# Favor attention and two expert layers on one core: the later units' projections by heads, with the high and the low part stacked in the partitions

## Chip, core and metric

The kernel runs on one core of a Trainium2 chip. The metric is the device time in microseconds (us) of one execution; lower is better. The engines are named as in the profile: PE is TensorE's matmul side and PEld its weight loads, DVE is VectorE, ACT ScalarE, POOL GpSimd, SP the queue from which most transfers are issued.

## The reference

Three stages follow each other; the second and third take the first one's result. Only the first is touched. Inputs q, k, v have 4 batches, 8 heads, 576 tokens and 64 numbers per token and head; omega is 128 x 64.

```python
def phi(x):                                   # x: q or k, times 64 ** -0.25
    proj = np.einsum('bhsd,md->bhsm', x, omega)
    sq = np.sum(x * x, axis=-1, keepdims=True) / 2.0
    h = proj - sq
    h = h - np.max(h, axis=-1, keepdims=True)
    return np.exp(h) / np.sqrt(m)
q_p, k_p = (phi(q_s), phi(k_s))
kv = np.einsum('bhsm,bhsd->bhmd', k_p, v)
z = np.sum(k_p, axis=2)
num = np.einsum('bhsm,bhmd->bhsd', q_p, kv)
den = np.einsum('bhsm,bhm->bhs', q_p, z)[..., None] + 1e-06
return (num / den).astype(np.float32)
```

After it come a gated layer over all 2304 tokens (512 to 1536 to 512) and a layer of 8 experts (512 to 1024 to 512) in which each token goes to one expert.

## The kernel before

Attention is cut into 72 units: one unit is 128 tokens of q or of k, four heads each. The first 16 units ("start") and the next 14 are put in order by a planner (`Plan`); the 42 after them, the later units, are not planned: `start_unit` puts their steps into a list of tasks with due times (`T.at`, `SOFFS`), and the loop of the gated layer (`moe1_group`, `T.step`) lets each task out between its own products. So a later unit's products stand in TensorE's queue among the long products of the gated layer: `gv`, 384 columns, and `acc`, 512 columns. The order is fixed when the program is built.

The steps of a unit are made by `unit_stages`. `s1` transposes the 128 tokens by two matmuls (a transpose takes two heads of 64 numbers, so the result has two heads above each other in the 128 partitions) into the PSUM tile `xt`, [128, 2, 128]. To keep float32 precision with the faster rounded type (F32R), `s1b` copies `xt`, rounded, to `xh` on ScalarE, and `s1x` subtracts it from `xt` on VectorE, which leaves the low part `xl`. `s1c` makes the sums of squares. `s2` is the projection: for each pair of heads, `mm3` (lines 186 to 189) issues three products, high by high, high by low, low by high:

```python
o = pr[:, 2 * a:2 * a + 2, :].rearrange("p h m -> p (h m)")
mm3(o, xh[:, a, :], xl[:, a, :], om_h, om_l, True, True)
```

Since a pair has two heads in the partitions, `om_h` and `om_l` (128 x 256, the high and low part of omega) hold omega twice: in partitions 0 to 63 for the columns 0 to 127, in partitions 64 to 127 for the columns 128 to 255, and zeros elsewhere. A pair's products have 256 columns, and half of what they multiply is zeros. `s2b` (maximum, VectorE) and `s2c` (exponential, ScalarE) read the result `pr`; the rest of a unit (`s3...`, `s4...`, `s5...`) is the attention itself. `xt`, `pr`, `qt`, `num` and `xot` of later units share two PSUM buffers (`misc`); `xh` and `xl` have one buffer each.

Units are numbered from 0 to 71 here; unit 30 is the first later one. Each later unit's `s2` issues 6 products of 256 columns.

Of the kernel before, what the change touches and what calls it, by code (L numbers as in the profile page):

```python
# [8 lines left out]
F32 = mybir.dt.float32  # L9
F32R = mybir.dt.float32r  # L10
I32 = mybir.dt.int32
ACTF = mybir.ActivationFunctionType
ALU = mybir.AluOpType
# [46 lines left out]
P = 128  # L60
# [79 lines left out]
def kernel(  # L140
# [16 lines left out]
    nc = tc.nc  # L157
# [25 lines left out]
    def misc(shape, name):  # L183
        return psum.tile(shape, F32, tag="misc", name=name, bufs=2)

    def mm3(o, lh, ll, rh, rl, start, stop):
        nc.tensor.matmul(o, lh, rh, start=start, stop=False, skip_group_check=True)  # L187
        nc.tensor.matmul(o, lh, rl, start=False, stop=False, skip_group_check=True)  # L188
        nc.tensor.matmul(o, ll, rh, start=False, stop=stop, skip_group_check=True)  # L189
# [11 lines left out]
    with tc.manual_schedule():  # L201
        upool = ctx.enter_context(tc.tile_pool(name="upool", bufs=2))
        tpool = ctx.enter_context(tc.tile_pool(name="tpool", bufs=1))
        attn = attn_stack.enter_context(tc.tile_pool(name="attn", bufs=1))
# [62 lines left out]
        def load_x(n, x):  # L267
            kind, t, j = units[n]
            src = q if kind == "q" else k
            for r, m, b, s in segs(t):  # L270
                nc.sync.dma_start(out=x[r:r + m],
                                  in_=src[b, 4 * j:4 * j + 4, s:s + m, :].rearrange("h s d -> s h d"))
# [30 lines left out]
        def pump():  # L303
            while nload[0] < len(units) and room["xin"]:
                n = nload[0]
                room["xin"] -= 1
                loads[n] = attn.tile([P, 4, D], F32, tag="xin", name="xin", bufs=3)
                load_x(n, loads[n])
                nload[0] += 1
                if not planning:  # L310
                    pump_v()
            if not planning:
                pump_v()

        def pump_v():
            while nload[1] < nload[0]:
                n = nload[1]
                kind, t, j = units[n]
                if kind == "k":
                    nv = 1 + edge(t)  # L320
                    if room["vin"] < nv:
                        return
                    room["vin"] -= nv
                    vt = [attn.tile([P, 4, D + 2], F32, tag="vin", name="vin", bufs=2) for _ in range(nv)]
                    vals[n] = [x.rearrange("p (h b) d -> p h b d", b=2) for x in vt] if nv > 1 else vt[0]
                    load_v(n, vals[n])
                nload[1] += 1
# [16 lines left out]
        def first_tile(n):  # L344
            if n not in first:
                first[n] = wpool.tile([P, 1024], F32, tag="w", name="first")
            return first[n]
# [17 lines left out]
        def first_part(src, j, u):  # L365

            hp, rp = divmod(u, 2)
            return quad[src, j][:, 2 * hp:2 * hp + 2, 2 * rp:2 * rp + 2, :]
# [49 lines left out]
        om_h = const.tile([P, 2 * P], F32R, name="om_h")  # L418
        om_l = const.tile([P, 2 * P], F32R, name="om_l")
# [23 lines left out]
        def wsteps(key):  # L443

            st = {}


            def a():
                st["r"] = wraw.pop(key)
                st["t"] = rows.tile([P, DM], I32, tag="row", name="wt")  # L450
                nc.vector.tensor_scalar(out=st["t"], in0=st["r"][:, :, 1], scalar1=3, scalar2=0x3FFFFFFF,
                                        op0=ALU.logical_shift_left, op1=ALU.bitwise_and)

            def b():
                nc.vector.scalar_tensor_tensor(out=st["t"], in0=st["r"][:, :, 1], scalar=-0x40000000, in1=st["t"],
                                               op0=ALU.bitwise_and, op1=ALU.bitwise_or)

            def c():
                nc.vector.scalar_tensor_tensor(out=st["t"], in0=st["r"][:, :, 0], scalar=29, in1=st["t"],
                                               op0=ALU.logical_shift_right, op1=ALU.bitwise_or)  # L460

            def d():
                wch[key] = wpool.tile([P, 2, DM], F32R, tag="w", name="w")
                nc.scalar.copy(wch[key][:, 0, :], st["t"].bitcast(F32))

            def e():
                nc.vector.tensor_tensor(out=wch[key][:, 1, :], in0=st["t"].bitcast(F32),
                                        in1=wch[key][:, 0, :].bitcast(F32), op=ALU.subtract)

            return a, b, c, d, e  # L470
# [8 lines left out]
        def unit_stages(i):  # L479
            kind, t, j = units[i]  # L480
            x_none = kind == "k" and t < 4
            st = {}
            start = i < n_start
            planned = i < n_start + n_grp[0]
            accum = not start and planned

            def bank(shape, name):
                if i < n_start and name in ("xt", "xot"):
                    return psum.tile(shape, F32, tag="gv", name=name, bufs=2)
                if i < n_start and name == "pr":  # L490
                    return psum.tile(shape, F32, tag="acc", name=name, bufs=GT)
                return misc(shape, name)

            def s1():
                if start:
                    u = first_tile(i)
                    x = loads.pop(i, None)
                    xh = u[:, 4 * D:8 * D].rearrange("p (a t) -> p a t", t=P)
                    h = u[:, 8 * D:8 * D + 4 * M].rearrange("p (h m) -> p h m", m=M)
                else:  # L500
                    x = loads.pop(i)
                    h = attn.tile([P, 4, M], F32, tag="h", name="h", bufs=2)
                    xh = attn.tile([P, 2, P], F32R, tag="xh", name="xh", bufs=1)
                xl = None
                xt = bank([P, 2, P], "xt")
                if x is None:
                    part = first_part("k", j, t)
                    pair = [part[:, a].rearrange("p r d -> p (r d)") for a in range(2)]
                    hsq, xsq = h[:, :, 0:D].rearrange("p (a r) d -> p a r d", a=2), part
                else:  # L510
                    pair = [x[:, 2 * a:2 * a + 2, :].rearrange("p h d -> p (h d)") for a in range(2)]
                    hsq, xsq = h[:, :, 0:D], x
                for a in range(2):
                    nc.tensor.transpose(xt[:, a, :], pair[a], ident)
                ss = attn.tile([P, 4], F32, tag="ss", name="ss", bufs=4)
                st.update(x=x, xh=xh, h=h, ss=ss, xt=xt, pair=pair, sq=(hsq, xsq))

            def s1b():
                nc.scalar.copy(st["xh"], st["xt"])

            def s1x():
                xl = st["xl"] = attn.tile([P, 2, P], F32R, tag="xl", name="xl", bufs=1)
                nc.vector.tensor_tensor(out=xl, in0=st["xt"], in1=st["xh"].bitcast(F32), op=ALU.subtract)

            def s1c():
# [14 lines left out]
            def s2():  # L540
                xh, xl = st["xh"], st.get("xl")
                pr = st["pr"] = bank([P, 4, M], "pr")
                for a in range(2):
                    o = pr[:, 2 * a:2 * a + 2, :].rearrange("p h m -> p (h m)")
                    if start:
                        nc.tensor.matmul(o, xh[:, a, :], om_f, start=True, stop=True)
                    else:
                        mm3(o, xh[:, a, :], xl[:, a, :], om_h, om_l, True, True)
# [111 lines left out]
            def s5c():  # L660
                nc.vector.tensor_tensor(out=st["o"][1], in0=st["xo"], in1=st["o"][0].bitcast(F32), op=ALU.subtract)  # L661
                if not start:
                    freed("xin")

            parts = dict(T=s1, xh=s1b, xl=s1x, sq=s1c, pj=s2, rd=s2b, ex=s2c)
            if start:
                parts = dict(T=s1, xh=s1b, sq=s1c, ss=s1d, sc=s1e, pj=s2, rd=s2b, md=s2m, ex=s2c)
            elif accum:
                parts = dict(T=s1, xh=s1b, xl=s1x, sq=s1c, pj=s2, rd=s2b, md=s2m, ex=s2c)
# [87 lines left out]
        for g, n2, n3 in ((0, 4, 2), (1, 1, 1), (2, (NT - E) // (2 * P) + E, 0)):  # L757
            r = Round()
# [588 lines left out]
        for n, key in enumerate(worder):  # L1347
            load_chunk(n)
            st = wsteps(key)
# [113 lines left out]
        fin[3].extend(x for x in plan.todo if x[0] != "end")  # L1463
        plan.run(fin)
        planning.clear()
        pump()
        TG = NF * (4 * 0.98 + 3 * 0.65)
        p0 = T.now - TG
# [15 lines left out]
        st = slot_prefetch(A, A.slots[0], tf + PF, PD, tf + FR[0][0] * 12 + FR[0][1] + 1.4 + PG)  # L1484
        moe1_group(NG - 1)
        cur = pending[0]
        for i, (r, s) in enumerate(slots):
# [4 lines left out]
            st = nst  # L1492
# [53 lines left out]
```

## Time and profile before

| | us |
|---|---|
| median of 2 runs (872.6 to 872.7) | 872.65 |
| the profiled execution, its own time | 873.23 |
| its span, from the first to the last instruction | 871.30 |
| PE busy | 851.5 (98%) |
| PEld busy | 788.1 (90%) |
| DVE busy | 599.1 (69%) |
| ACT busy | 369.3 (42%) |

The profile's rows come from one profiled execution. Busy time of PE is the union of its products' durations; they overlap, because a product's row runs until its last result is written while the next one has long begun. What a product costs in a row of products is the distance between two starts. A weight load (LDWEIGHTS) brings a product's stationary operand into the array, and each product has one.

### The profile page before, as it was taken

To read this page: it belongs to the slowest core of one execution; us is meant where nothing else is said; L and a number is where in the kernel's file an instruction comes from. 1 tells how busy PE (TensorE), PEld (TensorE's weight loads), DVE (VectorE), ACT (ScalarE), POOL (GpSimd) and SP (SyncE) were. 2 spreads that over 40 slices of the span, in tenths; PEclk is the share of its full clock that TensorE was granted. 3 is DMA by queue.
4 is the path that set the end of the run, shared out by engine and by line. 5 is a ranking of instruction groups with operands and counts; after the bars stand their busy time and mean duration, and the time that the engine had idled before them with its cause. 6 is when DMAs were issued, how large, how long until landed. Compare 5 with 4: busy or idle time off the path is not lost. (4 is left out here: it accounts for less than half of the span.)

```text
span 871.3 us, 14616 instructions
## 1 busy us (share of the span) xinstructions
PE 851.5 (98%) x5115; PEld 788.1 (90%) x5115; DVE 599.1 (69%) x1581; ACT 369.3 (42%) x1024; POOL 101.0 (12%) x236
## 2 busy tenths in 40 slices
PE   7899999999999999999999999999999999999994
PEld 6789889999999999999999999999999999999994
DVE  6999899466665666566666665488887777976520
ACT  4857665334333434243443331211374445555420
POOL 6812200000000000000000000000112014321010
PEclk9999999999999999999999999999999999999998
DMA  8926641222213112141112211131767654776000
GB/s 254 277 76 183 215 140 43 76 50 59 63 46 111 38 42 55 43 133 43 37 43 77 51 32 37 57 113 46 260 220 278 200 182 140 253 246 233 25 27 25
DMA packets 89389, 98.68 MB, mean 113 GB/s; under 512 B 53504, under 2 KB 55570, under 8 KB 89307
## 3 DMA queue, kind: packets, MB, share of 16 engines
q1 hardware_dynamic: 85995, 87.90, 33.0%
q0 software_dynamic: 3040, 9.70, 3.2%
q8 instruction: 42, 0.69, 0.3%
q14 instruction: 40, 0.33, 0.1%
q10 hardware_dynamic: 272, 0.07, 0.0%
HBM read 84.26 MB, written 13.65 MB: 112 GB/s over the span
## 5 line engine op out<-in xcount | busy, mean ns | idle before, releaser
L187 PE MATMUL gv<-xT,w 128*128 128x384 f32 x576 | 201.4, 350 | 0.4 <-DVE xT L661 0.4
L189 PE MATMUL gv<-xT,w 128*128 128x384 f32 x576 | 193.9, 337 | 0.0
L188 PE MATMUL gv<-xT,w 128*128 128x384 f32 x576 | 193.5, 336 | 0.0
L187 PE MATMUL acc<-w,uh 128*128 128x512 f32 x352 | 143.6, 408 | 0.0
L189 PE MATMUL acc<-w,ul 128*128 128x512 f32 x352 | 138.8, 394 | 0.0
L188 PE MATMUL acc<-w,uh 128*128 128x512 f32 x352 | 138.7, 394 | 0.0
L578 ACT ACTIVATE h<-pr,mx 128x128 f32<-128x128 f32 x224 | 64.1, 369 | 145.1 <-DVE mx L573 133.4
L187 PEld LDWEIGHTS gv<-xT,w 128*128 128x128 f32 x576 | 108.4, 188 | 3.2 <-DVE xT L661 0.6
L188 PEld LDWEIGHTS gv<-xT,w 128*128 128x128 f32 x576 | 108.5, 188 | 2.4
L189 PEld LDWEIGHTS gv<-xT,w 128*128 128x128 f32 x576 | 108.1, 188 | 0.0
L788 DVE SCALAR_TENSOR_TENSOR wge<-xrow,wge 128x512 f32<-128x512 f32 x144 | 98.7, 685 | 11.4 <-DMA wge<-wg2t 10.7
L193 DVE TENSOR_TENSOR w<-raw,w 128x512 fp32r<-128x512 f32 x128 | 85.4, 687 | 3.2 <-ACT w L192 1.9
L189 PEld LDWEIGHTS acc<-w,ul 128*128 128x128 f32 x352 | 66.0, 188 | 14.6
L187 PE MATMUL h<-sx,w 128*128 128x256 f32 (+1 forms) x256 | 78.4, 306 | 0.0
L189 PE MATMUL h<-sx,w 128*128 128x256 f32 (+1 forms) x256 | 77.6, 303 | 0.0
L188 PE MATMUL h<-sx,w 128*128 128x256 f32 (+1 forms) x256 | 77.4, 302 | 0.0
L192 ACT CAST w<-raw 128x512 fp32r<-128x512 f32 x128 | 74.0, 618 | 2.0 <-DMA raw<-in_moe_w_dram 2.0
L188 PEld LDWEIGHTS acc<-w,uh 128*128 128x128 f32 x352 | 66.5, 189 | 7.5
L187 PEld LDWEIGHTS acc<-w,uh 128*128 128x128 f32 x352 | 66.4, 189 | 7.4
L560 DVE TENSOR_REDUCE mx<-pr 128x4 f32<-128x512 f32 x72 | 49.5, 687 | 22.9 <-PE pr L189 19.4
L1083 ACT CAST uh<-th 128x384 fp32r<-128x384 f32 x72 | 37.6, 522 | 63.6 <-DVE th L1078 62.3
L1074 DVE SCALAR_TENSOR_TENSOR th<-th,gv 128x384 f32<-128x384 f32 x72 | 39.7, 551 | 35.8 <-ACT th L1071 35.8
(232 smaller groups left out, 1409.3 us busy)
## 6 DMA issues: line engine op xcount, KB each, us to landing
raw<-in_moe_w_dram SPq DMA_DIRECT2D x64, 512.0 KB
wge<-wg2t SPq DMA_DIRECT2D x48, 256.0 KB
scr<-xrow SPq DMA_DIRECT2D x33, 256.0 KB
wraw<-in_moe_w_gate_dram SPq DMA_DIRECT2D x12, 512.0 KB
wraw<-in_moe_w_val_dram SPq DMA_DIRECT2D x12, 512.0 KB
wraw<-in_moe_w_out_dram SPq DMA_DIRECT2D x12, 512.0 KB
xin<-in_q_dram SPq DMA_DIRECT2D x26, 128.0 KB
xin<-in_k_dram SPq DMA_DIRECT2D x24, 128.0 KB
```

The lines of the kernel that those rows point to most:

```text
L187: nc.tensor.matmul(o, lh, rh, start=start, stop=False, skip_group_check=True)
L188: nc.tensor.matmul(o, lh, rl, start=False, stop=False, skip_group_check=True)
L189: nc.tensor.matmul(o, ll, rh, start=False, stop=stop, skip_group_check=True)
L192: nc.scalar.copy(hi, src)
L193: nc.vector.tensor_tensor(out=lo, in0=src, in1=hi.bitcast(F32), op=ALU.subtract)
L560: nc.vector.tensor_reduce(out=mx, in_=pr, axis=AX.X, op=ALU.max)
L578: nc.scalar.activation(out=h[:, a, :], in_=pr[:, a, :], func=ACTF.Exp, bias=mx[:, a:a + 1])
L788: nc.vector.scalar_tensor_tensor(out=st[e][:, 1, :], in0=xrows[i], scalar=1.0, in1=st[e][:, 0, :], op0=ALU.mult, op1=ALU.mult, accum_out=L ...
L1074: nc.vector.scalar_tensor_tensor(out=th[f], in0=th[f], scalar=1.0, in1=ps.pop((f, "g")), op0=ALU.add, op1=ALU.mult)
L1083: nc.scalar.copy(u[f][0], th[f])
```

## The change

The later units (not `planned`) get one tile `xs`, [128, 2, 2, 128], F32R. Its second axis is the place r of a head within the pair. For r = 0 the high part of the head in partitions 0 to 63 stays in partitions 0 to 63, and its low part is written to partitions 64 to 127; for r = 1 it is the other way round. So `xs[:, r, a, :]` holds one head, high and low above each other, and one product with omega's high part in both halves of the partitions gives (high + low) by omega's high part. `s1b` becomes two copies of 64 partitions, `s1x` two subtractions of 64 partitions whose result lies in the other half of the partitions, and `s2` eight products of 128 columns: for each of four heads one with `om_h` and one with `om_l`. For that, ScalarE copies omega's second block over the zeros beside it in `om_h` and `om_l` once, behind the planned part. The 30 units before keep their products; the 14 planned later ones only have `xh` and `xl` in the two halves of the new tile.

```diff
-                    xh = attn.tile([P, 2, P], F32R, tag="xh", name="xh", bufs=1)
+
+                    xh = st["xs"] = attn.tile([P, 2, 2, P], F32R, tag="xs", name="xs", bufs=1)
+                    if planned:
+                        xh = xh[:, 0]
...
             def s1b():
-                nc.scalar.copy(st["xh"], st["xt"])
+                if planned:
+                    nc.scalar.copy(st["xh"], st["xt"])
+                    return
+                for r in range(2):
+                    here = slice(64 * r, 64 * r + 64)
+                    nc.scalar.copy(st["xh"][here, r], st["xt"][here])
 
             def s1x():
-                xl = st["xl"] = attn.tile([P, 2, P], F32R, tag="xl", name="xl", bufs=1)
+                if not planned:
+                    for r in range(2):
+                        here, there = slice(64 * r, 64 * r + 64), slice(64 - 64 * r, 128 - 64 * r)
+                        nc.vector.tensor_tensor(out=st["xh"][there, r], in0=st["xt"][here],
+                                                in1=st["xh"][here, r].bitcast(F32), op=ALU.subtract)
+                    return
+                xl = st["xl"] = st["xs"][:, 1]
                 nc.vector.tensor_tensor(out=xl, in0=st["xt"], in1=st["xh"].bitcast(F32), op=ALU.subtract)
...
                 pr = st["pr"] = bank([P, 4, M], "pr")
+                if not planned:
+                    for a in range(2):
+                        for r in range(2):
+                            for n in range(2):
+                                nc.tensor.matmul(pr[:, 2 * a + r, :], xh[:, r, a, :], (om_h, om_l)[n][:, 0:P],
+                                                 start=n == 0, stop=n == 1)
+                    return
...
         planning.clear()
+
+        for om in (om_h, om_l):
+            nc.scalar.copy(om[64:128, 0:P], om[64:128, P:2 * P].bitcast(F32))
         pump()
```

The order of everything else on the five engines' queues is the same as before. Three places show what is new, all at unit 30. The first is TensorE's queue at its projection, between products of the gated layer (gv); before:

```order
L189 MATMUL gv<-xT_1604,w 128x384
L187 MATMUL pr<-om_h,xh 128x256 [waits DVE_49,Activation_49]
L188 MATMUL pr<-om_l,xh 128x256
L189 MATMUL pr<-om_h,xl 128x256 [waits DVE_49]
L187 MATMUL pr<-om_h,xh 128x256
L188 MATMUL pr<-om_l,xh 128x256
L189 MATMUL pr<-om_h,xl 128x256
L187 MATMUL gv<-xT_1604,w 128x384
```

And the same place of TensorE's queue with the change:

```order
L189 MATMUL gv<-xT_1594,w 128x384
L561 MATMUL pr<-om_h,xs 128x128 [waits DVE_49]
L561 MATMUL pr<-om_l,xs 128x128
L561 MATMUL pr<-om_h,xs 128x128 [waits DVE_49,Activation_49]
L561 MATMUL pr<-om_l,xs 128x128
L561 MATMUL pr<-om_h,xs 128x128
L561 MATMUL pr<-om_l,xs 128x128
L561 MATMUL pr<-om_h,xs 128x128
L561 MATMUL pr<-om_l,xs 128x128
L187 MATMUL gv<-xT_1594,w 128x384
```

Six products of 256 columns became eight of 128; the low part, which only the third product waited for, is now wanted by the first, and the second half of the low part by the third. The second place is VectorE's queue at the same unit's subtraction, with the change (before, one row `L523 TENSOR_TENSOR xl<-xt,xh 128x256` stood there, and it waited for ScalarE):

```order
L1099 SCALAR_TENSOR_TENSOR th<-th,gv 128x384 [waits DVE_49]
L1107 TENSOR_TENSOR ul<-th,uh 128x384 [waits Activation_49]
L533 TENSOR_TENSOR xs<-xt,xs 64x256 [waits PE_49,Activation_49]
L533 TENSOR_TENSOR xs<-xt,xs 64x256
L550 TENSOR_REDUCE ss<-h 128x4 [waits Activation_49,Pool_49]
L581 TENSOR_REDUCE mx<-pr 128x4 [waits PE_49]
```

There are two subtractions in a row, and only the first has a wait for ScalarE. The third place is ScalarE's queue just ahead of that, with the change (before, one row `L519 CAST xh<-xt 128x256` stood for the two of xs, and none for omega):

```order
L1104 CAST uh<-th 128x384 [waits DVE_49,PE_49]
L1489 CAST om_h<-om_h 64x128
L1489 CAST om_l<-om_l 64x128
L527 CAST xs<-xt 64x256 [waits PE_49]
L527 CAST xs<-xt 64x256
L549 ACTIVATE h<-xin 128x4x64 [waits DMAHW6_49]
```

The copies within omega came in once, and each later unit has two copies for one.

## Rows read from the trace of the kernel before

**Rows 1.** The profile's page: span, busy time and share of each engine, 40 slices.
```profile
span 871.3 us, 14616 instructions
PE 851.5 (98%) x5115; PEld 788.1 (90%) x5115; DVE 599.1 (69%) x1581; ACT 369.3 (42%) x1024; POOL 101.0 (12%) x236
```

**Rows 2.** Length, busy us (instructions) of PE, PEld, DVE, ACT, POOL in two stretches, then granted clock and DMA.
```profile
155.00:520.00 365.00, 364.88 (x2269) 343.94 (x2268) 230.45 (x668) 138.24 (x403) 3.45 (x30) 1.00 0.22 59
520.00:835.00 315.00, 315.00 (x1786) 289.60 (x1785) 223.62 (x600) 126.44 (x254) 43.15 (x57) 1.00 0.48 159
```

**Rows 3.** Waits, 155 to 520 us: who waited for whom, us, times, longest.
```profile
DVE xl L523 <- ACT xh L519: 35.7, 35, 2.1
...
PEld xt L514 <- DVE xT L661: 0.5, 2, 0.2
```

**Rows 4.** Tile pr, 155 to 520 us: ns min/median/max, first and last start.
```profile
L188 PEld LDWEIGHTS pr<-om_l,xh x84: 187/188/193, 161.9 to 509.5; 128*128 128x128 f32 x84
...
L189 PE MATMUL pr<-om_h,xl x84: 278/281/297, 162.1 to 509.7; 128*128 128x256 f32 x84
```

**Rows 5.** Timeline of PE at a later unit's projection: start us, duration us, instruction.
```profile
309.98 0.28 PE L187 MATMUL pr<-om_h,xh 128*128 128x256 f32 x1
...
310.70 0.39 PE L187 MATMUL acc<-w,uh 128*128 128x512 f32 x1
310.93 0.40 PE L188 MATMUL acc<-w,uh 128*128 128x512 f32 x1
```

**Rows 6.** Timeline of PE in the routing, three products of 42 columns among long ones.
```profile
614.19 0.34 PE L188 MATMUL gv<-xT,w 128*128 128x384 f32 x1
...
614.54 0.41 PE L1026 MATMUL inv<-f_mv,f_lh 128*128 128x42 f32 x3
...
615.05 0.34 PE L188 MATMUL gv<-xT,w 128*128 128x384 f32 x1
```

**Rows 7.** The weight loads of the same place.
```profile
614.76 0.19 PEld L187 LDWEIGHTS gv<-xT,w 128*128 128x128 f32 x1
614.87 0.19 PEld L188 LDWEIGHTS gv<-xT,w 128*128 128x128 f32 x1
```

**Rows 8.** Timeline of PE, four products (passes) of 130 columns among long ones.
```profile
250.97 0.61 PE L614 MATMUL part<-vin,h 128*128 128x130 f32 x4
...
251.59 0.33 PE L188 MATMUL gv<-xT,w 128*128 128x384 f32 x1
```

**Rows 9.** Timeline at unit 30: start us, duration us, instruction [idle before it <- releaser].
```profile
161.02 0.38 ACT L519 CAST xh<-xt 128x256 fp32r<-128x256 f32 x1 [0.55 <-PE xt L514]
...
161.42 0.42 DVE L523 TENSOR_TENSOR xl<-xt,xh 128x256 fp32r<-128x256 f32 x1 [0.37 <-ACT xh L519]
...
161.88 0.28 PE L187 MATMUL pr<-om_h,xh 128*128 128x256 f32 x1
```

**Rows 10.** Groups by line and form, 0 to 20 us: the form of 64 partitions.
```profile
L416 ACT ACTIVATE om_f<-omT 64x128 f32<-64x128 f32 x2 | 0.5, 272 | 2.5 <-PE omT L412 2.5
```

**Rows 11.** Timeline of ScalarE and VectorE at the unit of Rows 5.
```profile
307.18 0.37 ACT L519 CAST xh<-xt 128x256 fp32r<-128x256 f32 x1 [0.64 <-PE xt L514]
307.45 0.42 ACT L535 ACTIVATE h<-xin 128x256 f32<-128x256 f32 x1
...
307.58 0.42 DVE L523 TENSOR_TENSOR xl<-xt,xh 128x256 fp32r<-128x256 f32 x1 [1.86 <-ACT xh L519]
307.93 0.41 DVE L536 TENSOR_REDUCE ss<-h 128x4 f32<-128x256 f32 x1
```

**Rows 12.** Timeline at a unit with little time between subtraction and projection.
```profile
277.06 0.42 DVE L523 TENSOR_TENSOR xl<-xt,xh 128x256 fp32r<-128x256 f32 x1 [1.21 <-ACT xh L519]
...
277.85 0.28 PE L187 MATMUL pr<-om_h,xh 128*128 128x256 f32 x1
```

**Rows 13.** Line 1026 over the whole span: ns min/median/max, first and last start, forms.
```profile
L1026 PE MATMUL inv<-f_mv,f_lh x33: 172/257/267, 614.5 to 772.2; 128*128 128x18 f32 x18, 128*128 128x42 f32 x15
```

**Rows 14.** Tile gv, 155 to 520 us, one of its three lines.
```profile
L187 PE MATMUL gv<-xT,w x343: 331/334/445, 155.3 to 519.6; 128*128 128x384 f32 x172
```

## The prediction

> **What bounds the kernel now.** I read the page first: TensorE is busy 98% of the span, and the weight loads beside it are busy 90%, VectorE 69%, ScalarE 42% [rows 1]. An average says little about one stage, so I then cut the span by what runs in it. The changed instructions are those of the 42 later units; the table of their projections runs from 161.9 to 509.7 us [rows 4]. In the stretch 155 to 520 us TensorE is busy 364.88 of 365.00 us, from 520 to 835 us all 315.00 of 315.00 us, at the full granted clock in both; VectorE is busy 230.45 and ScalarE 138.24 of the 365 us [rows 2]. In the list of waits of that first stretch, TensorE's products have no entry, and the longest entry of the weight loads is 0.5 us in two waits [rows 3]. So time that is added to TensorE's queue there, or taken from it, moves the end by the same amount: nothing behind it up to 835 us has a hole that could take it in. What counts is the spacing of starts on TensorE, not the durations: two neighbouring products overlap in the rows.
>
> **What the six products cost now.** A later unit's projection is two times three products of 256 columns. The first starts at 309.98 us, the next product of another kind at 310.70 us: 0.72 us for six, 0.120 us each [rows 5]. The spacing grows with the columns: 0.175 us for 384 (two from 614.19 to 614.54 us [rows 6]) and 0.23 us for 512 (310.70 to 310.93 us [rows 5]), about 0.055 us for each 128 columns over a base of some 0.01 us. At 256 columns the moving side still sets the spacing, just. A straight line would give 0.064 us for 128 columns, and eight of these would be 0.51 us: that is the gain the change could be read to have.
>
> **What eight products of 128 columns cost.** No product of 128 columns of this type stands in the trace, so I take the nearest rows. In the routing, three products of the same rounded type with 42 columns stand between long ones. From the first at 614.54 us to the second long one after them at 615.05 us are 0.51 us; one long one takes 0.175, so the three take 0.335 us, 0.112 each [rows 6], although 42 columns on the line above would take a quarter of that. The weight loads say why: after the three the next two start at 614.76 and 614.87 us, 0.11 us apart [rows 7]. A load of 128 x 128 starts when the product before it has started, and the next product then waits for it; a short product no longer covers it. Four products of 130 columns (plain f32, two passes of the array) show the same: 250.97 to 251.59 us less one long one of 0.175 are 0.445 us, 0.111 each [rows 8], though each streams more than twice as long. From 42 to 130 columns the price is 0.11 us, so it is the load's and not the columns'. Every product brings its own load: of the six now, the second has the same stationary operand as the first and is still loaded, 84 times [rows 4]. So eight products cost 8 x 0.112 = 0.894 us, and the unit grows by 0.894 - 0.72 = 0.174 us. The change takes a third of the columns away (1024 for 1536) and adds a third of the loads (8 for 6), and at this width the loads are what is paid for. 42 x 0.174 = **+7.3 us**.
>
> The Trainium skill, "TensorE: Matmul & The Clock Gate", section "LDWEIGHTS (loading the stationary operand)", says that a load's time goes by its columns, P / 1.2 ns, which is an estimated 107 ns for 128; these rows agree, with 0.11 us. By it alone eight would be 0.853 us, and the sum 42 x 0.133 = 5.6 us.
>
> **The other engines.** ScalarE's one copy of 128 x 256 becomes two of 64 x 256, VectorE's one subtraction likewise. The row nearest to half the partitions is ScalarE's 64 x 128 form, 272 ns [rows 10], against 0.37 us for the copy of 128 x 256 and 0.42 us for the subtraction [rows 11]; that shows no saving by partitions that I could take, so each half costs between 0 and a whole, and I take a whole. On its engine an instruction takes less than its duration, for the next one starts before it ends: after a copy at 307.18 us the next starts at 307.45, after a subtraction at 307.58 us the next at 307.93 [rows 11]. So 42 x 0.27 = 11.3 us are added to ScalarE's 138 and 42 x 0.35 = 14.7 us to VectorE's 230 of 365 us [rows 2]. Both stay far from full. The two copies into om_h and om_l (of the 64 x 128 form, 0.27 us each) stand on ScalarE ahead of unit 30's first copy, which comes at 161.02 us after 0.55 us of idle time: they fit into that [rows 9].
>
> What can reach TensorE is the latency of the chain. By the order, the first subtraction waits for ScalarE and the second waits for nothing more; I take it that the wait is for both copies. Then the first subtraction ends 0.27 us later than the single one did and the second 0.27 + 0.35 = 0.62 us later. The cover is the time between the subtraction's end and the projection's start. In the unit shown it is 309.98 - 308.00 = 1.98 us [rows 5, 11]. The least are unit 30's, 161.88 - 161.84 = 0.04 us [rows 9], and 277.85 - 277.48 = 0.37 us [rows 12] at a unit whose third product, 0.22 us on, is the one that wants the second half. So unit 30 stalls by up to 0.4 us, and others at most by a few hundredths: **+0.4 us** in all. The chain behind the projection (maximum, exponential) starts 0.174 us later, but whoever waits for it stands behind the same products on TensorE and is late by as much.
>
> **The sum.** 7.3 + 0.4 = 7.7 us. The profiled execution's span of 871.3 us [rows 1] becomes 879.0, its time of 873.23 us 880.9. The median of the runs shown is 0.6 us under the profiled time, so the forecast is 872.65 + 7.7, about **880.3 us**, 0.9% slower.
>
> **Rivals.**
> Loads that hide under short products (faster). If the eight products ran at the line's 0.064 us, the unit would shrink by 0.72 - 0.51 = 0.21 us and the kernel by 8.7 us, to 864 us. For it speaks that the operands now are alike in pairs. Against it stands the price of 0.11 us at both 42 and 130 columns [rows 6, 8]. Chance 0.04. The Trainium skill's page named above, section "Back-to-back issue gap", gives 81 ns for a product of 128 columns in a stream of load and product pairs; 42 x (8 x 0.081 - 0.72) would be -3.0 us (869.6 us), an estimate; these rows, with 0.11 us, do not agree with it.
>
> Narrow products of this type run at a quarter of the rate (slower by over 2%). Then 128 columns would take what 512 take now, 0.23 us [rows 5], the unit 1.84 us, and 42 x 1.12 = 47 us would be added: 920 us. The spacing of the 42-column products can't exclude it, since four times 42 columns still fit under a load. Their durations speak against it: the medians of 281 ns at 256 columns [rows 4] and 334 ns at 384 [rows 14] make a column 0.414 ns, by which 18 columns would last 182 ns, and 205 ns at a quarter of the rate; the shortest of the 33 products in that line, of which 18 have 18 columns, is 172 ns [rows 13]. Ends of products are modelled, so that is no proof. Chance 0.05.
>
> The chain's cover is used up (slower). If the half copies and subtractions delay every projection, not unit 30's alone, each 0.1 us of stall in all 42 adds 4.2 us; the whole 0.62 us would add 26 us (906 us); over 2% it goes from 0.24 us a unit beside the 0.174. Against it: VectorE waited for the copy in 35 of the 42 subtractions, 35.7 us in all, so there is no backlog in front of them [rows 3]. Chance 0.05, mostly below 890 us.
>
> Nothing moves: the added time falls into a hole, and it stays at 872 to 874 us. That needs idle time on TensorE, and there is 0.12 us of it in 155 to 520 us [rows 2]. Chance 0.03.
>
> **How the numbers follow.** The forecast has 0.83, with its own range of 878.5 to 882.5 us (0.107 to 0.115 us for a product is 5.7 to 8.4 us, with 0 to 1.5 us of stalls). The range for 8 in 10 is 877.5 to 884 us: it leaves out both far rivals and takes in a little more stall. A change of under about 2% is what a measurement of this kernel can't tell from none: faster by more needs over 17 us, which not even hidden loads give (0.01); slower by more comes from the quarter rate and from the far end of the chain rival (0.05 + 0.01); within 2% the rest, 0.93.
>
> **What would show it.** In the profile after, 336 products of 128 columns with 336 loads in 155 to 530 us; the first of a unit's eight to the next long product 0.89 us; busy TensorE without holes to the end of the stretch; the last projection some 7 us later than 509.7; one wait of about 0.4 us at unit 30. Wrong would be: a spacing of 0.06 us (hidden loads), of 0.23 us (quarter rate), or a row of waits of these products for VectorE.

## The result and the profile after

The changed kernel takes 883.05 us (median of two runs, 882.93 to 883.17) for 872.65: a ratio of 1.0116, with a 95% interval of 1.0100 to 1.0133, which is 10.1 us more (8.7 to 11.6). The forecast was 880.3 us in a range of 877.5 to 884.0. So the direction and the range held, and the size was off by a quarter of what was measured: 10.4 us between the medians for 7.7 forecast. The time lies just outside the narrower range of 878.5 to 882.5 us that the prediction gave for its own forecast.

| | before | after |
|---|---|---|
| median of the runs | 872.65 us | 883.05 us |
| profiled execution, its span | 873.23, 871.3 us | 883.17, 881.2 us |
| granted clock, mean of the span | 0.99 | 0.99 |
| TensorE products, busy | 5115, 851.5 us | 5199, 861.4 us |
| ScalarE, VectorE busy | 369.3, 599.1 us | 390.4, 620.6 us |

The page of the changed kernel, which answers to [rows 1]:

```profile
span 881.2 us, 14949 instructions
PE 861.4 (98%) x5199; PEld 795.5 (90%) x5199; DVE 620.6 (70%) x1623; ACT 390.4 (44%) x1068; POOL 100.6 (11%) x236
```

The same cut by stage as [rows 2], with borders moved by the 10 us; the columns are the length, busy us (instructions) of PE, PEld, DVE, ACT and POOL, then the granted clock, the DMA share and GB/s:

```profile
155.00:530.00 375.00, 374.22 (x2352) 351.34 (x2351) 251.67 (x710) 159.09 (x446) 3.42 (x30) 1.00 0.21 58
530.00:845.00 315.00, 314.95 (x1784) 289.06 (x1783) 223.52 (x599) 126.53 (x254) 42.93 (x57) 1.00 0.48 159
```

The stage from 530 us on is what it was from 520 us on. The stage of the 42 later units is 10 us longer, and two things are new in it: TensorE works longer, and it has 0.78 us without any product, for 0.12 us before. (That is less than it stalls: a short product counts as busy for 0.28 us where starts follow every 0.11 us, so only the end of a wait shows as a hole.) The list of waits of that stage says where (who waited for whom, us in all, times, longest):

```profile
PEld pr L561 <- DVE xs L533: 1.2, 3, 0.6
PEld xt L517 <- DVE xT L682: 0.8, 3, 0.3
PEld pr L561 <- issue: 0.7, 3, 0.2
```

In [rows 3] no wait of a projection (pr) stood. Now its loads wait for VectorE's subtractions (xs, L533). Tile pr in this stage, as in [rows 4]:

```profile
L561 PE MATMUL pr<-om_h,xs x168: 221/274/327, 162.0 to 519.3; 128*128 128x128 f32 x168
L561 PE MATMUL pr<-om_l,xs x168: 272/275/278, 162.2 to 519.4; 128*128 128x128 f32 x168
```

These are the 336 products of 128 columns, the last at 519.4 us where the last of before was at 509.7. At a unit without a wait, TensorE's timeline, with the first two weight loads (PEld), shows the price of the eight (start us, duration us; answers to [rows 5]):

```profile
314.69 0.33 PE L189 MATMUL gv<-xT,w 128*128 128x384 f32 x1
314.70 0.19 PEld L561 LDWEIGHTS pr<-om_h,xs 128*128 128x128 f32 x1
314.87 0.22 PE L561 MATMUL pr<-om_h,xs 128*128 128x128 f32 x1
314.87 0.19 PEld L561 LDWEIGHTS pr<-om_l,xs 128*128 128x128 f32 x1
314.93 0.28 PE L561 MATMUL pr<-om_l,xs 128*128 128x128 f32 x1
315.04 0.28 PE L561 MATMUL pr<-om_h,xs 128*128 128x128 f32 x1
...
315.59 0.28 PE L561 MATMUL pr<-om_l,xs 128*128 128x128 f32 x1
315.71 0.44 PE L187 MATMUL acc<-w,uh 128*128 128x512 f32 x1
315.99 0.40 PE L188 MATMUL acc<-w,uh 128*128 128x512 f32 x1
```

From the second product on a start follows every 0.11 us. The first is followed after 0.06 us: its own load had started under the long product ahead (314.70), so its successor's load could start with it (314.87). Those 0.06 us are about the time that 128 columns stream, for in the run with products of 64 columns below the same gap is 0.03 us. The debt is paid at the end, where the first long product is followed after 0.28 us and not after 0.23. From 314.87 to 315.71 are 0.84 us, and with the 0.05 behind it 0.89 us: the 0.894 us of the prediction.

At unit 30 it is another picture (ScalarE, VectorE and TensorE; in brackets the idle time ahead of an instruction and what ended it; answers to [rows 9]):

```profile
160.76 0.74 ACT L527 CAST xs<-xt 64x256 fp32r<-64x256 f32 x2
...
161.54 0.88 DVE L533 TENSOR_TENSOR xs<-xt,xs 64x256 fp32r<-64x256 f32 x2 [0.74 <-ACT xs L527]
...
161.44 0.34 PE L189 MATMUL gv<-xT,w 128*128 128x384 f32 x1
162.01 0.33 PE L561 MATMUL pr<-om_h,xs 128*128 128x128 f32 x1 [0.23 <-DVE xs L533]
162.17 0.28 PE L561 MATMUL pr<-om_l,xs 128*128 128x128 f32 x1
162.56 0.30 PE L561 MATMUL pr<-om_h,xs 128*128 128x128 f32 x1
...
163.26 0.39 PE L187 MATMUL gv<-xT,w 128*128 128x384 f32 x1
```

From the last long product ahead (161.44) to the first behind (163.26) are 1.82 us; undisturbed, from 314.69 to 315.71, they are 1.02. So unit 30 stalls by 0.80 us, once at its first product and again at its third, which wants the second half of the low part. (The load of the third starts at 162.53 us, 0.11 us after the second subtraction ends; the list puts these three waits down to "issue", which means that the profile shows no releaser.) The unit with the next least time to spare, that of [rows 12], stalls in the same way:

```profile
280.90 0.87 DVE L533 TENSOR_TENSOR xs<-xt,xs 64x256 fp32r<-64x256 f32 x2 [1.34 <-ACT xs L527]
...
281.08 0.40 PE L189 MATMUL acc<-w,ul 128*128 128x512 f32 x1
281.37 0.33 PE L561 MATMUL pr<-om_h,xs 128*128 128x128 f32 x1
281.54 0.28 PE L561 MATMUL pr<-om_l,xs 128*128 128x128 f32 x1
281.92 0.30 PE L561 MATMUL pr<-om_h,xs 128*128 128x128 f32 x1
...
282.62 0.45 PE L187 MATMUL acc<-w,uh 128*128 128x512 f32 x1
```

TensorE's products stand in the same order in both traces, so their starts can be set beside each other one by one. From 155 us on the changed kernel falls behind by 42 x 0.174 = 7.3 us at the projections, by a further 2.4 us at the projections of eight units (counted from 0 as in the prediction: unit 30 0.79, 41 0.28, 44 0.45, 45 0.15, 46 0.09, 56 0.45, 57 0.10, 58 0.08), and by 0.8 us at transposes that wait; it gains back 0.4 us where the states (kv) are no longer waited for, and it had come to 155 us 0.25 us ahead. Together that is 9.9 us at 520 us. Another 0.5 us is lost in the gated layer at 571 to 576 us and gained back behind the last product, so the spans differ by 9.9 us too. The 7.3 are the forecast; the stalls are the error.

### The profile page after: what moved, and what is told of

It is laid out like the page before. It is cut to its first block, busy times and chain, and to the rows that moved or that the text cites. A ratio compares the mean times of both kernels' runs of the same rounds, so it can differ in the third digit from the quotient of the medians.

```text
span 881.2 us, 14949 instructions
## 1 busy us (share of the span) xinstructions
PE 861.4 (98%) x5199; PEld 795.5 (90%) x5199; DVE 620.6 (70%) x1623; ACT 390.4 (44%) x1068; POOL 100.6 (11%) x236
## 5 line engine op out<-in xcount | busy, mean ns | idle before, releaser
L599 ACT ACTIVATE h<-pr,mx 128x128 f32<-128x128 f32 x224 | 63.9, 369 | 142.8 <-DVE mx L594 101.4
L533 DVE TENSOR_TENSOR xs<-xt,xs 64x256 fp32r<-64x256 f32 x84 | 35.5, 422 | 43.7 <-ACT xs L527 42.5
L1095 DVE SCALAR_TENSOR_TENSOR th<-th,gv 128x384 f32<-128x384 f32 x72 | 39.7, 551 | 35.5 <-ACT th L1092 35.2
```

What stands on the lines that cost most here:

```text
L533: nc.vector.tensor_tensor(out=st["xh"][there, r], in0=st["xt"][here], in1=st["xh"][here, r].bitcast(F32), op=ALU.subtract)
L599: nc.scalar.activation(out=h[:, a, :], in_=pr[:, a, :], func=ACTF.Exp, bias=mx[:, a:a + 1])
L1095: nc.vector.scalar_tensor_tensor(out=th[f], in0=th[f], scalar=1.0, in1=ps.pop((f, "g")), op0=ALU.add, op1=ALU.mult)
```

## The experiments

Each is set against runs of the kernel before on the same chip (medians of 872.4 to 872.8 us). In us, the last column is the ratio less one times 872.7, with the ends of its interval.

| | median | ratio, 95% interval | more than before |
|---|---|---|---|
| the change | 883.05 | 1.0116, 1.0100 to 1.0133 | 10.1 (8.7 to 11.6) |
| eight products, chain of before | 880.22 | 1.0087, 1.0071 to 1.0104 | 7.6 (6.2 to 9.1) |
| chain in halves, products of before | 876.46 | 1.0045, 1.0028 to 1.0062 | 3.9 (2.4 to 5.4) |
| sixteen products of 64 columns | 918.53 | 1.0525, 1.0508 to 1.0543 | 45.8 (44.3 to 47.4) |
| eight products with zeros | 883.79 | 1.0127, 1.0110 to 1.0144 | 11.1 (9.6 to 12.6) |
| transposes and chain earlier | 885.71 | 1.0146, 1.0129 to 1.0162 | 12.7 (11.3 to 14.1) |
| projections later | 892.05 | 1.0215, 1.0198 to 1.0232 | 18.8 (17.3 to 20.2) |
| the change, whole copies | 881.56 | 1.0099, 1.0082 to 1.0116 | 8.6 (7.2 to 10.1) |
| extra chain, 128 partitions | 873.79 | 1.0012, 1.0002 to 1.0021 | 1.0 (0.2 to 1.8) |
| extra chain, partitions 0 to 63 | 874.10 | 1.0011, 1.0001 to 1.0020 | 1.0 (0.1 to 1.7) |
| extra chain, partitions 64 to 127 | 875.50 | 1.0032, 1.0021 to 1.0043 | 2.8 (1.8 to 3.8) |

**My theory** was: a short product costs its load, so two more products are +7.3 us, and the rest is the low part that comes too late for some projections. **The rivals**: the columns count after all; or VectorE and ScalarE, with 42 more instructions each, are what is short; or the lateness can simply be scheduled away.

### The products alone

The chain of copy and subtraction as before, and eight products of 128 columns:

```diff
+                if not planned:
+                    for a in range(2):
+                        for r in range(2):
+                            for n in range(2):
+                                nc.tensor.matmul(pr[:, 2 * a + r, :], (xh, xl)[n][:, a, :],
+                                                 om_h[:, r * P:(r + 1) * P], start=n == 0, stop=n == 1)
+                    return
```

> The kernel before, with its copy, subtraction and tiles, but eight products of 128 columns for its six of 256: for each head high by high and low by high. The product high by low is left out, so that there are eight. Theory: the loads alone, 42 x 0.174 = 7.3 us, 880.0 us, and no new waits of the projections. Rival (the products are late because of the chain in front of them, and the eight cost no more than six): 873 us.

Measured: 880.22 us, and the stage of the later units is full: TensorE is busy 370.00 of the 370.00 us from 155 to 525 us. The price of the products stands alone here, and it is that of the prediction (7.3 us at the projections when the traces are set beside each other). The list of waits of this stage has no line of a projection; its first is that of the kernel before with 0.1 us less [rows 3]:

```profile
PEld xt L514 <- DVE xT L668: 0.4, 2, 0.2
```

### The chain alone

The six products of before, and copy and subtraction in halves of 64 partitions that stay in their own partitions:

```diff
+                for r in range(2):
+                    here = slice(64 * r, 64 * r + 64)
+                    nc.scalar.copy(st["xh"][here], st["xt"][here])
...
+                for r in range(2):
+                    here = slice(64 * r, 64 * r + 64)
+                    nc.vector.tensor_tensor(out=xl[here], in0=st["xt"][here], in1=st["xh"][here].bitcast(F32),
+                                            op=ALU.subtract)
```

> The kernel before with its six products of 256 columns, but the copy and the subtraction of the later units in two halves of 64 partitions each, as the change has them. Theory: the halves run one behind the other without overlap, so the low part comes 0.8 us later; units 30, 44 and 56, with 0.04 and 0.37 us of cover, stall by some 0.2 to 0.6 us each and their neighbours by 0.1: 1 to 2.5 us in all, 873.7 to 875.2 us. Rival (the rest of the 10.4 us has nothing to do with the chain): 872.7 us.

Measured: 876.46 us, more than I expected. Its list of waits from 155 to 530 us:

```profile
PEld xt L514 <- DVE xT L672: 1.7, 5, 0.5
PEld pr L189 <- DVE xl L533: 1.4, 4, 0.6
```

About half of it are projections that wait for the low part, in four units. The other half are transposes (xt) that wait for VectorE's xT; in [rows 3] they did so for 0.5 us, here for 1.7. So the added instructions make late not only what they produce but also what stands behind them on their engine. At the longest of these waits, at 498.59 us, VectorE runs from the subtractions (491.67) to the unit's maximum (495.06) with one hole of 0.27 us; the exponentials follow the maximum, and xT follows them on ScalarE. Products and chain together, 7.6 + 3.9 = 11.5, are the 10.1 of the change within the intervals.

### Columns or loads: half the columns, and twice the columns

Each product of the changed kernel cut into two of 64 columns:

```diff
+                            for c in (slice(0, 64), slice(64, 128)):
+                                for n in range(2):
+                                    nc.tensor.matmul(pr[:, 2 * a + r, c], xh[:, r, a, :], (om_h, om_l)[n][:, c],
+                                                     start=n == 0, stop=n == 1)
```

> The changed kernel with each product of 128 columns cut into two of 64: 16 products a later unit, the columns together the same 1024. Theory (a short product costs its weight load, 0.112 us, whatever its columns): 16 x 0.112 = 1.79 us a unit for 0.893, so 42 x 0.894 = 37.5 us more than the changed kernel, 920.5 us, and starts 0.11 us apart. Rival (0.112 us is what 128 columns of this type take, at half the rate): 64 columns take 0.056 us, the unit stays near 0.9 us and the time near 883 to 885 us.

Measured: 918.53 us, 35.5 more than the change with the same columns. TensorE's timeline:

```profile
330.02 0.19 PE L562 MATMUL pr<-om_h,xs 128*128 128x64 f32 x1
330.05 0.27 PE L562 MATMUL pr<-om_l,xs 128*128 128x64 f32 x1
330.16 0.28 PE L562 MATMUL pr<-om_h,xs 128*128 128x64 f32 x1
330.27 0.28 PE L562 MATMUL pr<-om_l,xs 128*128 128x64 f32 x1
```

Products of 64 columns are 0.11 us apart, like those of 128; only the first, whose load is ready, is followed sooner (0.03 us). The 35.5 are less than the 37.5 expected because stalls went away: the sixteen products themselves add the 37.5 us, but the stalls at projections shrink from 2.4 to 1.0 us and no transpose xt is left in the list of waits. The other way round, the kernel before with a fourth product of 256 columns a pair, zeros and all:

```diff
-                        mm3(o, xh[:, a, :], xl[:, a, :], om_h, om_l, True, True)
+                        mm3(o, xh[:, a, :], xl[:, a, :], om_h, om_l, True, planned)
+                        if not planned:
+                            nc.tensor.matmul(o, xl[:, a, :], om_l, start=False, stop=True, skip_group_check=True)
```

> The kernel before with a fourth product for each pair of heads in the later units, low part by low part of omega: eight products of 256 columns with the zeros kept, and the chain of copy and subtraction as before. It computes one small term more than either kernel. If a product costs its load and not its columns, two more products of 0.12 us in each of 42 units give +10.1: 882.5, and the blocks of zeros cost only 8 x (0.120 - 0.112) = 0.07 us a unit, 2.8 us in all beside the run with eight products of 128 columns (880.2). If the columns counted, eight products of 256 columns would cost twice eight of 128: with 0.89 us a unit for those, 1.79, which is +45 and 917.

Measured: 883.79 us. Against the eight products of 128 columns with the same chain (880.22) that is 3.6 us for 42 x 1024 columns less. At the projections alone the traces show 2.7 us, for 2.8 expected. So with the count of products held fixed the zeros are worth some 3 us, and eight products for six cost about 10 us with the zeros kept and 7.3 without them: the count is what the change pays for.

### Whether the stalls can be scheduled away

The table of due times, with the transposes, copies, subtractions and squares of the later units 0.9 us earlier:

```diff
+        SOFFS.update(dict.fromkeys(("T", "xh", "xl", "sq"), -0.9))
```

> The changed kernel with the later units' transposes, copies, subtractions and squares due 0.9 us earlier in the list of tasks; the projections stay where they are. Theory: the chain's 0.8 us are covered again, the stalls at the projections (2.4 us by the aligned traces) are gone and the 7.3 us of loads remain: 880 to 881 us. Rival (the loads cost more than worked out and the waits are only where it shows): no change, 883 us.

Measured: 885.71 us. This missed. The stalls at the projections did go, all but unit 30's, but others came in the list of waits:

```profile
PEld qt L648 <- DVE xT L682: 3.2, 7, 0.5
PEld xt L517 <- ACT h L599: 3.0, 10, 0.5
...
PEld pr L561 <- DVE xs L533: 0.5, 1, 0.5
```

The transposes (xt, qt) now stand ahead of what they need: xt waits for ScalarE's exponentials (h, L599) in ten places, qt for VectorE's xT in seven. Neither reads what it waits for; what they want is a PSUM buffer, since xt, pr, qt and xot share two. The other way, the projection and what reads it 0.9 us later:

```diff
+        SOFFS.update(dict.fromkeys(("pj", "rd", "ex"), OFFS[1] + 0.9))
```

> The changed kernel with one more line in the planner's table: the projection (and the reads of the maximum and the exponentials that follow it) is due 0.9 us later than before, so that other TensorE work stands between a unit's transposes and its products. Nothing is left out. If the stalls at the projections (2.4 us over units 30, 41, 44, 45, 46, 56, 57 and 58) come from the low part being 0.83 us later, they go, and nothing else is disturbed: 880.5 to 881.5. If the slack is missing everywhere, so that a later projection only hands the wait to the steps behind it, as in the run with the earlier transposes: 883 or more, with new waits at qt or xt.

Measured: 892.05 us, the second branch of what was expected:

```profile
PEld qt L648 <- ACT h L599: 7.3, 14, 0.9
...
PEld pr L561 <- DVE xs L533: 0.6, 1, 0.6
```

Again only unit 30's projection waits, and the transposes of the features (qt) wait for the exponentials (h, L599) in 14 places. In both tries, time that one step got was taken from the next.

### Why the chain is that late

In the changed kernel the low part is ready 1.65 us after the first copy starts; in the kernel before it was 0.82 [rows 11]. That is 0.83 us later, where I had worked out 0.62. ScalarE and VectorE at the unit of the timeline above without a wait:

```profile
312.06 0.76 ACT L527 CAST xs<-xt 64x256 fp32r<-64x256 f32 x2 [0.64 <-PE xt L517]
312.84 0.42 ACT L549 ACTIVATE h<-xin 128x256 f32<-128x256 f32 x1
...
312.85 0.42 DVE L533 TENSOR_TENSOR xs<-xt,xs 64x256 fp32r<-64x256 f32 x1 [1.88 <-ACT xs L527]
```

The two copies take 0.76 us, twice a whole one, and what follows starts only behind them; whole ones overlapped by 0.10 us [rows 11]. Four kernels ask what takes the overlap away. First the change with copies of all 128 partitions into both slots:

```diff
-                    here = slice(64 * r, 64 * r + 64)
-                    nc.scalar.copy(st["xh"][here, r], st["xt"][here])
+                    nc.scalar.copy(st["xh"][:, r], st["xt"])
```

> The changed kernel, but both copies take all 128 partitions of the transposed tile, into the two slots, and the subtractions then overwrite the halves that hold the low part; nothing is left out. If it is the change of the first partition from one instruction to the next that keeps neighbours from overlapping, the pair of copies takes about 0.27 + 0.38 = 0.65 us instead of 0.76, the subtractions still 0.86 to 0.88, and the low part comes 0.1 us earlier: some 0.3 us less than the changed kernel, 882.7. If instructions of 64 partitions are simply slower, the copies shrink alike; if copies never overlap, 0.76 stays and so does the time.

Measured: 881.56 us. The pair of copies takes 0.65 us, the subtractions 0.86 us as in the change:

```profile
311.26 0.65 ACT L526 CAST xs<-xt 128x256 fp32r<-128x256 f32 x2 [0.64 <-PE xt L517]
311.79 0.43 ACT L548 ACTIVATE h<-xin 128x256 f32<-128x256 f32 x1
...
311.94 0.86 DVE L532 TENSOR_TENSOR xs<-xt,xs 64x256 fp32r<-64x256 f32 x2 [1.87 <-ACT xs L526]
```

Two copies of twice the partitions are faster than the two halves. The gain of 1.5 us is larger than I expected (0.3), though the two intervals overlap. With the traces set beside each other, each of the eight stalls at projections is 0.1 us shorter, 0.7 us in all, and the transposes wait 0.6 us less. Then the kernel before, with one more copy and one more subtraction of the whole tile in each unit:

```diff
                 nc.scalar.copy(st["xh"], st["xt"])
+                if not planned:
+                    nc.scalar.copy(st["h"][:, :, D:2 * D], st["xt"].rearrange("p a (r d) -> p (a r) d", d=D))
...
+                if not planned:
+                    y = st["h"][:, :, D:2 * D]
+                    nc.vector.tensor_tensor(out=y, in0=st["xt"].rearrange("p a (r d) -> p (a r) d", d=D), in1=y,
+                                            op=ALU.subtract)
                 nc.vector.tensor_tensor(out=xl, in0=st["xt"], in1=st["xh"].bitcast(F32), op=ALU.subtract)
```

> The kernel before with its six products, and in each later unit one more copy of the whole transposed tile on ScalarE (behind the first) and one more subtraction of the whole tile on VectorE (ahead of the one that counts), into a part of the unit's h tile that is overwritten later; so as many instructions in the chain as the changed kernel has, but of 128 partitions. If whole instructions overlap (0.27 us apart on ScalarE, 0.35 on VectorE, as rows of the kernel before show for neighbours) the low part comes about 0.6 us later instead of 0.83, and the time stays below that of the chain in halves (876.5): 874 to 875.5. If the number of instructions decides and not their form, 876 to 877.

Measured: 873.79 us, 1.0 over the kernel before, where the halves cost 3.9, with as many instructions. So it is not their number. To tell the size of 64 partitions from the place where they begin, the extra copy and subtraction were made of partitions 0 to 63 (`[0:64]` in the lines above), and then of 64 to 127 (`[64:128]`):

> The kernel before with one more copy and one more subtraction in each later unit, as in the run with whole ones, but these extra instructions take 64 partitions, 0 to 63; what they write is overwritten later. All four of the chain then begin at partition 0. If what keeps neighbours from overlapping is that they begin at other partitions, these overlap: second copy 0.27 us behind the first, second subtraction 0.34 behind the first, and the time is that of the run with whole instructions, 873.8 (873.3 to 874.5). If instructions of 64 partitions overlap with nothing, wherever they begin: copies 0.38 apart, subtractions 0.43 apart, and 875 to 876.5, near that of the chain in halves.

> The same as the run before it, but the extra copy and the extra subtraction take partitions 64 to 127, while the ones that count begin at partition 0. If the first partition decides: 0.38 us from copy to copy, 0.43 from subtraction to subtraction and from the second to what follows, the low part 0.2 us later than with partitions 0 to 63, and 875 to 876.5, near the chain in halves (876.5). If only the number of partitions decides, the same as with partitions 0 to 63.

Measured: 874.10 and 875.50 us. With partitions 0 to 63:

```profile
307.64 0.37 ACT L519 CAST xh<-xt 128x256 fp32r<-128x256 f32 x1 [0.64 <-PE xt L514]
307.91 0.36 ACT L521 COPY h<-xt 64x256 f32<-64x256 f32 x1
...
308.31 0.42 DVE L527 TENSOR_TENSOR h<-xt,h 64x256 f32<-64x256 f32 x1 [2.05 <-ACT h L521]
308.65 0.41 DVE L529 TENSOR_TENSOR xl<-xt,xh 128x256 fp32r<-128x256 f32 x1
```

With partitions 64 to 127:

```profile
308.53 0.37 ACT L519 CAST xh<-xt 128x256 fp32r<-128x256 f32 x1 [0.64 <-PE xt L514]
308.93 0.37 ACT L521 COPY h<-xt 64x256 f32<-64x256 f32 x1
...
309.33 0.43 DVE L527 TENSOR_TENSOR h<-xt,h 64x256 f32<-64x256 f32 x1 [1.93 <-ACT h L521]
309.77 0.42 DVE L529 TENSOR_TENSOR xl<-xt,xh 128x256 fp32r<-128x256 f32 x1
```

Same operations, same sizes: 0.27 us from copy to copy and 0.34 from subtraction to subtraction where all begin at partition 0; 0.40 and 0.44 where the first partition changes. It is the place, on both engines. (What follows the second subtraction came 0.34 us behind it, not the 0.43 expected: both begin at partition 0.) On ScalarE it is the change of place and not the upper half as such, for the two copies of omega in the changed kernel, which both begin at partition 64, overlap; no such pair was measured on VectorE:

```profile
160.23 0.30 ACT L1489 CAST om_h<-om_h 64x128 fp32r<-64x128 f32 x1
160.44 0.29 ACT L1489 CAST om_l<-om_l 64x128 fp32r<-64x128 f32 x1
```

For VectorE the Trainium skill, "VectorE: DVE Perf Modes", section "Two Vector instructions with no wait between them", has a model of this: an instruction starts only when every earlier VectorE instruction has finished if an input or its output begins in another group of 32 partitions than the last one in the same memory did. These rows agree with that sentence of the Trainium skill, with 0.44 us for 0.34.

From the start of the first copy to the end of the low part it is 0.82 us before, 1.42 and 1.43 us with the extra chain at partition 0 or of all partitions, 1.64 in halves, 1.66 with the extra chain at 64. The prices beside them are 0, 1.0, 1.0, 3.9 and 2.8 us: 0.6 us later is mostly covered, 0.8 us later is not.

## Why the prediction was right, and where it fell short

**What bounds the kernel.** That TensorE's queue is full in this stage, and that time added to it moves the end by as much, held: the products alone cost 7.6 us for 7.3, and no hole took any of it.

**The price of a short product.** 0.112 us, taken from products of 42 and of 130 columns, was right for 128 and for 64. The two far rivals fell with it: hidden loads would have been seen as 0.06 us from start to start, a quarter rate as 0.23, and where the load is ready a product of 128 columns takes 0.06 us and one of 64 takes 0.03. "Nothing moves" fell with the 10.1 us. The 81 ns of the Trainium skill, "TensorE: Matmul & The Clock Gate", section "Back-to-back issue gap", is not what these rows show, at 0.11 us.

**The stall term failed in size.** The forecast had 0.4 us, nearly all at unit 30; the change costs 2.5 us beyond its products (10.1 - 7.6, about 2 us either way by the intervals), and its trace shows 2.4 us at projections and 0.8 at transposes. The step that failed is the sentence "On its engine an instruction takes less than its duration, for the next one starts before it ends". It took 0.27 and 0.35 us for each added instruction from whole neighbours, and the halves do not overlap: 0.38 and 0.43, and the instruction after them waits as well. So the first half of the low part came 0.39 us later and not 0.27, the second 0.83 and not 0.62. The busy times say the same: VectorE's grew by 21.5 us where 14.7 had been worked out, ScalarE's by 21.1 where it was 11.3 and the two copies of omega. The hint stood in [rows 10]: two instructions of 272 ns are busy for 0.5 us together, so those, one on each half, do not overlap either. I read the duration there and not the sum.

**The covers were listed too briefly.** The run with whole extra instructions has just the 0.6 us that I had assumed. It costs 1.0 us, in an interval of 0.2 to 1.8 that takes in the 0.4; but its trace shows 0.8 us at projections, 0.49 at unit 30 and 0.15 at each of units 44 and 56. The prediction took the least two covers (0.04 and 0.37 us) and wrote that others stall "by a few hundredths". It followed the third product in the one unit it looked at, and did not go through all 42, of which eight stalled; nor did it count what stands behind the added instructions on VectorE and is waited for by transposes. Of its own signs, the 336 products and the 0.89 us came, but TensorE has holes of 0.78 us, the last projection comes 9.7 us later and not 7, and the row of waits for VectorE, named as a sign of being wrong, is there in part: three waits of 1.2 us in all.

**The rival of the used-up cover** was thus partly right: it was given 0.05 and put at every unit. Since the covers are unlike, the truth lay between, at eight units of 42.

One remark of the prediction was too wide: that a change under 2% can't be told from none. The interval of two runs tells 1.2% from none.

What stays open is part of the 0.8 us at transposes. At three of them (197.3, 506.1 and 522.7 us, 0.5 us together) VectorE runs from the unit's subtractions to the division or maximum that is waited for with at most one hole of 0.27 us, so it is its longer queue. The other 0.3 us are spread over small waits and were not traced to a cause.

## What to carry to other kernels

Count loads before columns: on a full TensorE a product of 128 columns or less, with a load of 128 x 128, costs 0.11 us here however narrow it is (42, 64 and 128 columns were seen), so in this kernel taking zeros out pays only if the number of products does not rise (eight with zeros 883.8, eight without 880.2, six with zeros 872.7 us). When a whole-tile instruction is cut into halves of partitions, price each half at a full duration, and the one behind them too, since a change of the first partition stops the overlap; then check every unit's slack with that figure, not the least one alone. In a schedule that is fitted end to end, moving a late step earlier or its consumer later can hand the wait on: neither try here gained anything by it, and they came out 2.6 and 8.7 us slower than the change (the interval of the first just overlaps the change's).

## What was not expected of the hardware

ScalarE, too, loses the overlap of neighbours when the first partition changes: 0.40 us from start to start in place of 0.27, for a copy of 64 x 256. A pair of copies of all 128 partitions is therefore cheaper than a pair of the two halves (0.65 us for 0.76). The loss also reaches one instruction further: behind the copy that begins at 64, two activations that both begin at partition 0 stand 0.45 us apart (309.32 to 309.77), and 0.32 (308.18 to 308.50) where the copy begins at 0. The second of them is the next to read PSUM; that this is the reason is not shown. And a stall costs TensorE a little more than the wait: after one, the first product of 128 columns is followed after 0.16 us and not 0.06 (162.01 to 162.17, 281.37 to 281.54 us). Its own load starts only with it there, and its successor's load 0.11 us later (162.12 and 281.48).
